# A recurrent attention layer feeding a two-matrix feed-forward layer: four reorderings in the opening stage

## The chip, the cores and the metric

The kernel runs on one core of one Trainium2 chip. The metric is device time in microseconds, the median of several executions. The engines of the core are called PE (TensorE, the matrix engine; PEld is its weight loading), DVE (VectorE), ACT (ScalarE), POOL (GpSimd) and SP (SyncE, which here only issues transfers). Each runs its own instructions strictly in the order of the program and waits at an instruction until what it needs is there. SP, ACT and POOL each have a queue of transfers of their own, and all queues are served by the same 16 DMA engines.

## The reference

```python
for t in range(S):                     # B=4, H=8, S=768, D=48
    cur = einsum('bhd,bhe->bhde', u[None] * kt, vt)
    y[:, :, t] = einsum('bhd,bhde->bhe', rt, state + cur)
    state = w[None, :, :, None] * state + einsum('bhd,bhe->bhde', kt, vt)
x = y.transpose(0, 2, 1, 3).reshape(B * S, H * D)   # 3072 x 384
h = x @ w_in                                        # 384 x 2048
out = (h * sigmoid(h)) @ w_out                      # 2048 x 384
```

A linear attention keeps one 48x48 state for each batch and head. The state is multiplied by `w` at every step and gets the outer product of `k` and `v`; the current step counts with the bonus `u` in place of the decay. The result goes through a feed-forward layer with a SiLU between its two matrices.

## The kernel before

**Units.** The sequence is cut into 6 chunks of 128 steps. A unit is one chunk of one batch: 24 units, numbered so that units 0 to 3 are the first chunk of the four batches. Inside a chunk the recurrence is written as matrix products, and only the state goes from chunk to chunk.

**Steps of a unit.** In the order text each step has a short name, with the unit's number behind it:

- `lr`, `lk`, `lv` load r, k and v (tiles `rin`, `kin`, `vin`), through SP's queue, 192 KB each (L73). For units 0 to 3 they are issued before the order begins.
- `T` turns r and then k on PE, by 8 small float32 transposes each (L251), into one of two large PSUM tiles `att`. `rT` and `kT` (L257, DVE) multiply the turned r and k by powers of w on the way out of PSUM.
- `A` is the product of r with k for two units at once (L284, PE, 64 float32 matmuls). It begins with a part of the even unit, and takes turns between the two units after that. `am` (L291, DVE) applies the causal mask.
- `ku`, `ru` (L211, L215, POOL), `rd` (L224, DVE) and `vu` (L229, POOL) make the bonus term: k times u, times r, summed over a head, times v.
- `v16` (L238, ACT) casts v to 16 bits; odd units also copy the two halves of it crosswise (`vx`, L241, L242).
- `Y` (L301, L306, PE) is the output, and `y16` (L334, DVE) adds the bonus term and casts. `yT` (L372, PE) and `xT` (L376, ACT) turn the output for the feed-forward layer.
- `kc` (L219, POOL), `S` (L318, PE) and `st` (L345, or L348 and L349, DVE) make the new state.

**The feed-forward layer.** `L` is a piece of the first product (L387, PE), `G` its SiLU (L395, ACT). The second product (L408) and the stores come later. `i_q` requests a quarter of w_in and `i_o` one of w_out, through POOL's queue, 384 KB each after a cast from float32 to float16 in the transfer (L84, L89).

**What sets the order.** The first units, up to about 45 us, follow an order written out by hand, a text of step names that a loop reads word by word (the end of the listing). It puts the instructions of every engine and queue in order. A number and a star ahead of a word mean that so many zero matmuls (128x512, tile `zs`, L161) are put on PE ahead of that step; they compute nothing. After the text a loop over pairs of units takes over, with pieces of the feed-forward layer put between them; the change does not touch that loop.

**Around the change.** `wb` spreads w over the 128 partitions with a matmul of one row (L185), `lnwb` takes its logarithm (L188, ACT), and `lamC` (L191 to L194, ACT) makes powers of w, which `kc` needs, and loads the table for the SiLU. `pads` are 8 small copies on ACT (L155) that zero the unused columns of r and k of units 4 to 7. PSUM tiles of the feed-forward layer, of `zs`, `bc`, `yp`, `sp` and `yT` share four buffers.

Of the kernel before, what the change touches and what calls it, by code (L numbers as in the profile page):

```python
# [15 lines left out]
def kernel(  # L16
# [132 lines left out]
    lamC = cst.tile([128, H, D], FP)  # L149
# [295 lines left out]
    def piece(word, f):  # L445
# [17 lines left out]
    }  # L463
    order = """
        lnw eK lamK mx clear lr4 lk4 lv4 lr5 lk5 lv5 lr6 lk6 lv6 lr7 lk7 lv7 4*T0 ku0 rT0 kT0
        4*T1 rT1 kT1 v160 ru0 rd0 ku1 wb v161 A01 ru1 am0 rd1 vu0 lnwb i_q0 lamC pads am1 vu1
        4*Y0 y160 T2 kT2 2*Y1 y161 ku2 ru2 rT2 yT0 xT0 i_q1 yT1 xT1 v162 T3 kT3 rT3 ku3 ru3 rd2
        v163 4*A23 vu2 i_q2 rd3 vu3 am2 am3 L0.0 G0.0 L0.2 G0.2 Y2 y162 Y3 y163 kc0 yT2 xT2 L0.4
        G0.4 kc1 yT3 xT3 L0.6 G0.6 S0 st0 kc2 T4 kT4 rT4 kc3 L2.0 G2.0 S1 L2.2 G2.2 st1 ku4 v164
        L2.4 G2.4 S2 L2.6 G2.6 st2 ru4 i_q3 r164 L4.8 G4.8 S3 L4.9 G4.9 st3 rd4 ku5 L4.10 G4.10  # L470
        T5 kT5 rT5 L4.11 G4.11 vu4 ru5 i_o0 A45 rd5 am4 r165 v165 L4.12 G4.12 vu5 kc4 L4.13
        G4.13 am5 sd4 kc5 Y4 S4 y164 st4 L4.14 G4.14 sd5 i_o1 Y5 S5 y165 st5 L4.15 G4.15 yT4 xT4
        yT5 xT5 T6 kT6 rT6 ku6 ru6 i_o2 H0 H1 v166 r166 H2 H3 T7 kT7 rT7 ku7 i_o3 v167 r167 H4
        ru7 rd6 stb4 stb5
# [106 lines left out]
```

## Time and profile before

| what | value |
|---|---|
| median of 5 executions | 194.7 us (194.66 to 195.44) |
| profiled execution | 195.18 us, of which the span from first to last instruction is 193.4 us |
| PE busy | 183.3 us, 95% of the span |
| POOL, ACT, DVE busy | 120.3, 108.2, 102.8 us |
| PE busy from 0 to 10, 10 to 20, 20 to 30 us | 7.53, 8.51, 8.95 us |
| PE busy from 30 to 40, 40 to 50, 50 to 60 us | 9.24, 9.23, 10.00 us |
| a load of r, k or v | 192 KB, 4.2 to 4.3 us from issue to landing (median) |
| a quarter of w_in | 384 KB, 5.9 us from issue to landing (median) |

How to read the profile: a line of the timeline gives the start, the time taken, the engine, the line of the kernel, the operation, the tile written and the tiles read, and how many instructions are merged in it; in brackets stands how long the engine sat idle before it and what released it. The letters `SPq` and `POOLq` mark the issuing of a transfer, not the transfer itself. The row of tenths cuts the span into 40 slices of 4.8 us; a 9 is 90% or more. Matmuls are pipelined, so the times of merged ones can overlap with what follows.

### The profile page before, as it was taken

What the parts mean: (1) busy time and instruction counts of PE and PEld (TensorE: products, weight loads), DVE (VectorE), ACT (ScalarE), POOL (GpSimd) and SP (SyncE); (2) the same over time, 40 slices, a digit from 0 to 9 for tenths busy, and PEclk for the clock granted to TensorE, in tenths of its full rate; (3) what the DMA queues carried; (4) which work ended last, traced back from release to release, by engine and by line L of the source; (5) the groups of instructions that cost most, each with busy time, mean ns of one, the idle gap of its engine ahead of it and who ended that gap; (6) DMA issues with size and microseconds to landing.
All of it is one profiled execution on the core that took longest, in us unless ns stands there. A gap on an engine that the chain in (4) does not pass through costs nothing.

```text
span 193.4 us, 5592 instructions
## 1 busy us (share of the span) xinstructions
PE 183.3 (95%) x2290; PEld 117.0 (61%) x2290; DVE 102.8 (53%) x188; ACT 108.2 (56%) x211; POOL 120.3 (62%) x159
## 2 busy tenths in 40 slices
PE   7788898989999999999999999999999999999992
PEld 2454684677766876665566655656755657644561
DVE  6378879855772672673673574574564355200121
ACT  5296577768380592176791276791386780199200
POOL 8489994999999939829839839739748230000000
PEclk9999999999999999999999999999999999999999
DMA  5999999999769458278177287177386201310012
GB/s 96 192 202 177 209 186 191 148 206 217 130 135 181 137 110 199 63 157 180 36 149 161 61 181 168 34 138 163 80 188 143 44 0 44 111 51 0 11 74 81
DMA packets 90123, 24.35 MB, mean 126 GB/s; under 512 B 83313, under 2 KB 90098, under 8 KB 90098
## 3 DMA queue, kind: packets, MB, share of 16 engines
q1 hardware_dynamic: 84992, 20.46, 48.8%
q0 software_dynamic: 3712, 3.15, 11.2%
q10 hardware_dynamic: 1394, 0.40, 1.0%
q8 instruction: 18, 0.29, 0.6%
q14 instruction: 7, 0.06, 0.1%
HBM read 20.65 MB, written 4.72 MB: 131 GB/s over the span
## 4 chain that ended last, share of the span: by engine, by line
PE 76%; POOL 13%; issue 4%; DMA 3%; ACT 2%; DVE 1%; ACTq 0%; POOLq 0%
PE ops L408 33%; PE hps L387 27%; PE att L284 7%; PE att L251 4%; POOL ku L211 3%; POOL kc L219 3%; DMA u_bc<-in_u_dram 3%; POOL vu L229 3%; POOL rku_f L215 2%; PE yp L306 2%; PE yp L301 2%; PE sp L318 1%; POOL win L84 1%; ACT gT L395 1%; POOL sdec L329 0%
## 5 line engine op out<-in xcount | busy, mean ns | idle before, releaser
L387 PE MATMUL hps<-xT,win 128*128 128x512 f16 (+1 forms) x360 | 68.2, 337 | 0.7 <-ACT xT L376 0.5
L395 ACT ACTIVATE gT<-hps 128x512 f16<-128x512 f32 x96 | 56.2, 598 | 18.6 <-PE hps L387 16.5
L408 PE MATMUL ops<-wout,gT 128*128 128x384 f16 x384 | 66.6, 326 | 0.0
L408 PEld LDWEIGHTS <-gT 128*128 128x128 f16 x384 | 36.3, 98 | 23.3
L387 PEld LDWEIGHTS <-win 128*128 128x128 f16 x360 | 33.2, 98 | 24.2 <-issue 1.1
L229 POOL TENSOR_TENSOR vu<-vin,rku 128x384 f32<-128x384 f32 x24 | 19.8, 830 | 28.6 <-DVE rku L224 28.6
L414 ACT COPY osb<-ops 128x384 f32<-128x384 f32 x20 | 9.6, 479 | 43.6 <-PE ops L408 39.8
L291 DVE TENSOR_TENSOR am<-att,maskM 128x1024 f16<-128x1024 f32 x12 | 14.7, 1224 | 33.4 <-PE att L284 33.4
L211 POOL TENSOR_TENSOR ku<-kin,u_bc 128x384 f32<-128x384 f32 x24 | 24.1, 1005 | 3.0 <-DMA u_bc<-in_u_dram 2.5
L215 POOL TENSOR_TENSOR rku_f<-rin,ku 128x384 f32<-128x384 f32 x24 | 24.1, 1004 | 1.7
L219 POOL TENSOR_TENSOR kc<-kin,lamC 128x384 f16<-128x384 f32 x24 | 23.9, 1003 | 0.0
L257 DVE TENSOR_TENSOR rT<-att,lamR 112x512 f32<-112x512 f32 x24 | 16.4, 685 | 11.4 <-ACT gT L395 4.0
L284 PEld LDWEIGHTS att<-rT,kT 48*64 48x64 f32 x768 | 17.9, 133 | 6.4 <-issue 4.5
L284 PE MATMUL att<-rT,kT 48*64 48x128 f32 (+1 forms) x768 | 20.5, 248 | 1.0 <-DVE rT L257 0.8
L334 DVE TENSOR_TENSOR y<-yp,vu 128x384 f16<-128x384 f32 x24 | 13.3, 556 | 13.6 <-issue 4.8
L257 DVE TENSOR_TENSOR kT<-att,lamK 112x512 f32<-112x512 f32 x24 | 16.4, 682 | 3.5 <-PE att L251 3.5
L291 DVE TENSOR_TENSOR am<-att,maskX 128x1024 f16<-128x1024 f32 x12 | 14.6, 1214 | 0.0
L238 ACT CAST v<-vin 128x384 f16<-128x384 f32 x24 | 11.5, 511 | 5.0 <-DMA vin<-in_v_dram 5.0
L416 DVE COPY osb<-ops 128x384 f32<-128x384 f32 x4 | 2.2, 558 | 21.8 <-PE ops L408 21.8
L329 POOL TENSOR_TENSOR sdec<-st,wCT 112x384 f32<-112x384 f32 x16 | 13.2, 825 | 0.0
L224 DVE TENSOR_REDUCE rku<-rku_f 128x8 f32<-128x384 f32 x24 | 12.4, 544 | 1.0 <-POOL rku_f L215 1.0
L272 ACT CAST rT<-rT 112x512 f16<-112x512 f32 x20 | 12.4, 619 | 0.3 <-DVE rT L257 0.2
(60 smaller groups left out, 161.8 us busy)
## 6 DMA issues: line engine op xcount, KB each, us to landing
rin<-in_r_dram SPq DMA_DIRECT2D x24, 192.0 KB, 4.2
vin<-in_v_dram SPq DMA_DIRECT2D x24, 192.0 KB, 4.2
out_dram<-osb SPq DMA_DIRECT2D x24, 192.0 KB, 2.2
kin<-in_k_dram SPq DMA_DIRECT2D x23, 192.0 KB, 4.3
win<-in_moe_w_in_dram POOLq DMA_DIRECT2D x4, 384.0 KB, 5.9
wout<-in_moe_w_out_dram POOLq DMA_DIRECT2D x4, 384.0 KB, 6.9
xT<-y SPq DMA_TRANSPOSE x18, 2.3
kin<-in_k_dram ACTq DMA_DIRECT2D x1, 192.0 KB, 3.6
```

The source lines that it names most:

```text
L211: nc.gpsimd.tensor_tensor(out=L(i)["ku"], in0=kin[i % NIN][:, :, 0:D], in1=u_bc, op=ALU.mult)
L215: nc.gpsimd.tensor_tensor(out=L(i)["rku_f"], in0=rin[i % NIN][:, :, 0:D], in1=L(i)["ku"], op=ALU.mult)
L219: nc.gpsimd.tensor_tensor(out=kc[i % NIN][:, :, 0:D], in0=kin[i % NIN][:, :, 0:D], in1=lamC, op=ALU.mult)
L229: nc.gpsimd.tensor_tensor(out=L(i)["vu"], in0=vin[i % NIN], in1=L(i)["rku"].unsqueeze(2).broadcast_to([128, H, D]), op=ALU.mult)
L257: nc.vector.tensor_tensor(out=L(i)[key].rearrange("p g (y t) -> p y g t", y=2), in0=L(i)["t"][0:PR, :, x], in1=lam.rearrange("p g (y t) -> ...
L284: nc.tensor.matmul(a[e][o0:o0 + HC, j, p, c0:C], kT[r0:r0 + D, p, s0:s0 + HC], rT[r0:r0 + D, p, c0:C], start=True, stop=True)
L291: nc.vector.tensor_tensor(out=am.rearrange("p h g c -> p (h g) c"), in0=L(i)["a"].rearrange("p h g c -> p (h g) c"), in1=(maskX if crossed ...
L329: nc.gpsimd.tensor_tensor(out=L(i)["sdec"], in0=st[b], in1=wCT.unsqueeze(2).broadcast_to([PR, NP, PW]), op=ALU.mult)
L334: nc.vector.tensor_tensor(out=L(i)["y16"], in0=L(i)["y"], in1=L(i)["vu"], op=ALU.add)
L387: nc.tensor.matmul(hps[:, f, :], win[:, q, (ft + f) * 128:(ft + f + 1) * 128], xts[sc][:, q, b0:b0 + nb, :].rearrange("p b t -> p (b t)"), ...
L395: nc.scalar.activation(out=gts[sc][:, ft:ft + m, b0 * C:(b0 + nb) * C], in_=hpss[b0, ft], func=AF.Silu)
L408: nc.tensor.matmul(opss[b], gts[sc][:, ft, b * C:(b + 1) * C], wout[:, ft, :], start=(ft == 0), stop=(ft == NFT - 1))
```

## The change

Only the order text changes, in four places; no instruction computes anything else than before.

- `wb` moves from ahead of the first pair product `A01` to behind it. `lnwb` moves ahead of `vu0`, and `am0` stays ahead of it; on ACT the order is as before.
- The zero matmuls: 2 instead of 4 ahead of `T1`, 4 new ones ahead of `A01`, 3 instead of 4 ahead of `Y0`, 3 instead of 2 ahead of `Y1`. In sum there are two more.
- `i_q0`, the request for the first quarter of w_in, moves on POOL from behind `vu0` to a place behind `ku1` and ahead of `ru1`. On POOL's queue nothing else moves.
- `T3` moves on PE from behind `yT1` to between `yT0` and `yT1`; `T5` moves ahead of `L4.10`. `T2` keeps its place behind `Y0` on PE. DVE's order is the same in both kernels.

```diff
-        4*T1 rT1 kT1 v160 ru0 rd0 ku1 wb v161 A01 ru1 am0 rd1 vu0 lnwb i_q0 lamC pads am1 vu1
-        4*Y0 y160 T2 kT2 2*Y1 y161 ku2 ru2 rT2 yT0 xT0 i_q1 yT1 xT1 v162 T3 kT3 rT3 ku3 ru3 rd2
+        2*T1 rT1 kT1 v160 ru0 rd0 ku1 v161 i_q0 4*A01 wb ru1 am0 lnwb vu0 rd1 3*Y0 lamC pads am1
+        vu1 T2 y160 kT2 3*Y1 y161 ku2 ru2 rT2 yT0 xT0 T3 i_q1 kT3 rT3 yT1 xT1 v162 ku3 ru3 rd2
         v163 4*A23 vu2 i_q2 rd3 vu3 am2 am3 L0.0 G0.0 L0.2 G0.2 Y2 y162 Y3 y163 kc0 yT2 xT2 L0.4
         G0.4 kc1 yT3 xT3 L0.6 G0.6 S0 st0 kc2 T4 kT4 rT4 kc3 L2.0 G2.0 S1 L2.2 G2.2 st1 ku4 v164
-        L2.4 G2.4 S2 L2.6 G2.6 st2 ru4 i_q3 r164 L4.8 G4.8 S3 L4.9 G4.9 st3 rd4 ku5 L4.10 G4.10
-        T5 kT5 rT5 L4.11 G4.11 vu4 ru5 i_o0 A45 rd5 am4 r165 v165 L4.12 G4.12 vu5 kc4 L4.13
+        L2.4 G2.4 S2 L2.6 G2.6 st2 ru4 i_q3 r164 L4.8 G4.8 S3 L4.9 G4.9 st3 rd4 ku5 T5 kT5 rT5
+        L4.10 G4.10 L4.11 G4.11 vu4 ru5 i_o0 A45 rd5 am4 r165 v165 L4.12 G4.12 vu5 kc4 L4.13
```

## The prediction

> **What bounds the kernel now.** The page comes first: TensorE (PE) is busy 95% of the span, and the busy tenths show where the rest is lost.
>
> ```profile
> span 193.4 us, 5592 instructions
> PE 183.3 (95%) x2290; PEld 117.0 (61%) x2290; DVE 102.8 (53%) x188; ACT 108.2 (56%) x211; POOL 120.3 (62%) x159
> PE   7788898989999999999999999999999999999992
> DMA  5999999999769458278177287177386201310012
> ```
>
> Apart from the last slice, PE's holes lie in the first ten, of 4.8 us each, the stage that the diff edits; there the DMA engines are busy as well. From 50 us on PE never waits (10.00 us busy of 50 to 60), so a shift of the front is carried to the end unless a later wait absorbs it. The page's chain of waits names POOL in the front, but POOL waits 2.7 us for DVE before `vu` of unit 4 at 32.38, so I follow DVE back from there. First VectorE in order of time:
>
> ```profile
> 12.12 1.22 DVE L291 TENSOR_TENSOR am<-att,maskM 128x1024 f16<-128x1024 f32 x1 [1.20 <-PE att L284]
> ...
> 15.91 0.55 DVE L334 TENSOR_TENSOR y<-yp,vu 128x384 f16<-128x384 f32 x1
> 16.38 0.68 DVE L257 TENSOR_TENSOR rT<-att,lamR 112x512 f32<-112x512 f32 x1
> 17.49 0.69 DVE L257 TENSOR_TENSOR kT<-att,lamK 112x512 f32<-112x512 f32 x1 [0.43 <-PE att L251]
> 18.09 0.68 DVE L257 TENSOR_TENSOR rT<-att,lamR 112x512 f32<-112x512 f32 x1
> 18.69 0.54 DVE L224 TENSOR_REDUCE rku<-rku_f 128x8 f32<-128x384 f32 x1
> 19.66 0.55 DVE L224 TENSOR_REDUCE rku<-rku_f 128x8 f32<-128x384 f32 x1 [0.42 <-POOL rku_f L215]
> 20.43 1.23 DVE L291 TENSOR_TENSOR am<-att,maskM 128x1024 f16<-128x1024 f32 x1 [0.22 <-PE att L284]
> ```
>
> Then PE over the same stretch:
>
> ```profile
> 15.45 0.34 PE L372 MATMUL yT<-ident,y 128*128 128x128 f16 x3
> 16.51 0.34 PE L372 MATMUL yT<-ident,y 128*128 128x128 f16 x3 [0.72 <-DVE y L334]
> 16.79 0.44 PE L251 MATMUL att<-ident,rin 64*112 64x64 f32 x8
> 17.06 0.39 PE L251 MATMUL att<-ident,kin 64*112 64x64 f32 x8
> 17.38 1.04 PE L161 MATMUL zs<-idle 128*128 128x512 f16 x4
> 18.34 2.04 PE L284 MATMUL att<-rT,kT 48*64 48x128 f32 x64
> ```
>
> The reader sees a chain. T3 (16.79, 17.06) stands behind yT1, which waits for y161. kT3 waits 0.43 us for T3; rT3 ends at 18.77; the pair product A23 ends near 20.4; am2 starts there. After it come am3, Y3 (22.85), the transposes and first-layer pieces without a pause, S0 (24.97), and VectorE solid from 25.34 to rd4 at 31.74, kT5, rT5, A45, and on through waits of 0.2 to 0.5 us. So a shift of am2 should reach the end one for one.
>
> **The change, part by part.**
>
> *T3 ahead of yT1.* y161 and rT2 end at 16.46 and 17.06 on VectorE as before. If T3 can run at about 15.9, kT3 starts at 17.06 instead of 17.49 and A23 ends near 19.95. But am2 stands behind rd3, which POOL's `rku_f` (18.61 + 1.01) releases, and that ends at 20.2. Gain: 20.43 - 20.2 = 0.23 us at most. T3 is now also the first thing PE waits on, and yT1, xT1, four zero matmuls and A23 queue behind it; xT1 has cover, as it is wanted by L0.0 after A23.
>
> *The first w_in quarter, requested behind `ku` of unit 1.* The issue costs POOL 0.93 us. It moves from 12.46 to about 10.67, the end of that `ku`. ru1 and vu0 slide by 0.9 us: ru1 ends near 12.6, before rd1 at 13.26 wants it, and vu0 near 13.4, before y160 at 14.85. vu1 still waits for rd1 until 13.80 (the 0.50 us wait that the row below shows), so POOL from vu1 on stands where it stood. On the engines this is nothing. On the transfers it is not.
>
> ```profile
> 9.64 1.01 POOL L211 TENSOR_TENSOR ku<-kin,u_bc 128x384 f32<-128x384 f32 x1
> 10.73 1.01 POOL L215 TENSOR_TENSOR rku_f<-rin,ku 128x384 f32<-128x384 f32 x1
> 11.69 0.83 POOL L229 TENSOR_TENSOR vu<-vin,rku 128x384 f32<-128x384 f32 x1
> 12.46 0.93 POOL L84 DMA_DIRECT2D win<-in_moe_w_in_dram  x1
> 13.89 0.82 POOL L229 TENSOR_TENSOR vu<-vin,rku 128x384 f32<-128x384 f32 x1 [0.50 <-DVE rku L224]
> ```
>
> Counted by queue in the trace's packet records, SP's queue moves some 50 KB each quarter microsecond until 14.25. Then the w_in packets begin, 1.8 us after the issue, and SP's queue has 23, 5, 4, 4, 4, 4, 0, 0, 0, 0 KB in the next ten quarters and is back at 45 near 17.5. The shortfall is about 2.7 us of its time; around the quarters issued at 16.69 and 20.35 it is about 2.2. Loads run one after another there, about 1.0 us each: rin3 12.53 to 13.6, kin3 from 13.60, 95% of it by 15.15, and it landed at 16.0 (11.42 + 4.6), just ahead of T3.
>
> With the issue at 10.67 the burst begins near 12.5, before rin3 rather than near the end of kin3. kin3 would end about 14.6 without a burst; add 2.2 to 2.7 for the stop: 16.8 to 17.3, and 0.9 from last packet to landing as for vin2 (12.54 to 13.4) and kin4 (21.86 to 22.8): 17.7 to 18.2. T3's second half started at 17.06 without waiting; started at 17.9 it shifts kT3, rT3, A23 and am2 by 0.85 us. `ku` of unit 3 (17.52) also waits for kin3, 0.4 us, and POOL has the 2.7 us to give.
>
> Here a rule is weighed. The Trainium skill, "DMA: Bandwidth & Descriptors", section "Queues, rings and completion order", says that a DMA engine takes turns between queues packet by packet. With equal bytes per turn the loads would run at half speed: rin3 and kin3, 384 KB at 100 KB per us from 12.5, end at 16.4 and land at 17.3, a shift of +0.25. The trace shows SP's queue at a tenth, not at half, so I stay near the row: 17.9, with +0.8 for the sum.
>
> *Zero matmuls.* Four 128x512 cost 1.04 us with their tail, 0.22 each in a row (0.26 alone). Two fewer before T1: T1 waits for rin1 (PE idled 0.60 us there), so nothing is gained. Four before the first product: T1 ends at 9.14, they end near 10.15, and the half of A01 that closes it waits for kT1 until 10.46. Nothing, unless the clock is slow. Three instead of four before Y0, behind the spread of w (0.91 us): A01 ends 12.06, spread 12.95, zeros about 13.7; am0 ends 13.34, so Y0 goes from 13.40 to some 13.6. Y0, T2, three zeros and Y1 then end near 15.6, and y161 is not due on VectorE before 15.91. Hidden, by 0.3 us; without that cover the sum would be +0.3. T2 and kT2 keep their places on PE and DVE.
>
> *Spread behind the product.* lnwb follows at 13.0 instead of 11.79 and ScalarE's chain (lamC, table load 1.28, pads) slides by 1.2: xT0 at 17.1 for 15.93. Both xT are due only at L0.0, 20.3. kc0 needs lamC at 21.96. Nothing.
>
> *T5 ahead of L4.10.* kT5 starts at 32.33, when rd4 ends; T5 was done by 32.05. PE does the same work before A45 in either order, and A45 waits for rT5. Nothing.
>
> Sum: +0.8 us from kin3, bounds -0.23 (no delay) and +1.15 (landing at 18.2), plus nothing else. The profiled execution took 195.18 for its span of 193.4, 0.48 above the median of the five; it becomes 196.0, and the median 194.7 becomes 195.5.
>
> The clock is the second rule weighed. Four zeros took 1.91 us at 2.97 and 1.04 at 6.30: PE ran at half speed until about 6 us. The Trainium skill, "TensorE: Matmul & The Clock Gate", Part 1, gives windows of about 3.4 us, an idle one returning PE to half speed, and Part 4 says transposes do not count as busy. With T3 late, zeros and Y1 end near 15.6 and the next zeros come at 18.7: 3.1 us of transposes alone. By the rows here (2.0 us between Y1's end and the next zeros, at full speed throughout) nothing is lost; by the rule it is close. If lost, A23 takes 3.1 instead of 1.55 us: +1.55 more.
>
> **Rivals.**
> 1. *The load is late enough (likeliest), 195.5.* For it: the empty quarters above, and kin3 landing only 1.1 us before it is used. Own range 195.0 to 196.0.
> 2. *Not slower: kin3 lands by 16.6.* One place, T3; the price is am2's 0.23 us gain, 194.5. It decides where kin3 lands before 17.06. For it: the edit removes the 0.43 us wait that the row shows. Against it: even equal turns land it at 17.3.
> 3. *Equal turns or a short burst:* kin3 at 17.1 to 17.4, 194.9.
> 4. *The clock falls back* in that gap, or before the first product where zeros went: 195.5 + 1.55 = 197.
>
> **How the numbers follow.** Chances: 0.60, 0.13, 0.17, 0.10. A measurement of this kernel tells about 0.3%, 0.58 us: below 194.12 is faster, above 195.28 slower. Slower: 0.85 of case 1 (0.51), all of case 4 (0.10), and 0.02 of case 3: 0.63. Faster: half of case 2, for a gain that I have not seen: 0.07. Same: 0.30. The range from 194.4 to 196.4 holds cases 1 and 3 and half of case 2; what is left out is case 4 and the rest of case 2, some 17 in 100.
>
> **What would show it.** Right: w_in packets from about 12.5, kin3 landing near 17.9, PE idle before T3's second half for that DMA, kT3 near 18.3, am2 near 21.2, rd4 near 32.6, and every row from 50 us shifted alike. Wrong: T3 done by 16.6 and am2 near 20.2; zero matmuls at 0.43 each; a later wait that swallows the shift; or POOL, not VectorE, releasing `vu` of unit 4.

## The result

The changed kernel takes 196.5 us in the median of 43 executions (195.41 to 198.97); the kernel before, measured again with 80, takes 195.25 us (194.36 to 197.99). The ratio is 1.006 with a 95% interval of 1.0045 to 1.0075: 1.2 us slower (0.9 to 1.5). Medians here are over all executions; the ratios, here and below, leave out those that took over 1.5% more than the fastest of the same kernel, and are not quotients of the medians. The forecast was slower by 0.8, to 195.5, between 194.4 and 196.4. The direction came true; the time lies 0.1 us outside the range, partly because the median of the kernel before, 194.7 over five executions, is 195.25 over eighty.

The profile after: first the busy row of the page and its row of the granted clock (in tenths of full speed), with the clock row of the kernel before under them; then PE in order of time over the stretch shown in the prediction.

```profile
span 194.2 us, 5596 instructions
PE   7797899889999999999999999999999999999992
PEclk9879999999999999999999999999999999999998
```

```profile
PEclk9999999999999999999999999999999999999999
```

```profile
15.65 0.36 PE L306 MATMUL yp<-vx,am 128*128 128x48 f16 x8
16.06 0.34 PE L372 MATMUL yT<-ident,y 128*128 128x128 f16 x3
16.33 0.43 PE L251 MATMUL att<-ident,rin 64*112 64x64 f32 x8
17.96 0.43 PE L251 MATMUL att<-ident,kin 64*112 64x64 f32 x8 [1.19 <-DMA kin<-in_k_dram]
18.32 0.34 PE L372 MATMUL yT<-ident,y 128*128 128x128 f16 x3
18.50 1.03 PE L161 MATMUL zs<-idle 128*128 128x512 f16 x4
19.46 1.87 PE L284 MATMUL att<-rT,kT 48*64 48x128 f32 x64
```

T3's first half follows yT0 at once, as the order now says. Its second half waits 1.19 us for k of unit 3 and starts at 17.96; before, it started at 17.06. VectorE shows what hangs on it:

```profile
12.73 1.22 DVE L291 TENSOR_TENSOR am<-att,maskM 128x1024 f16<-128x1024 f32 x1 [2.34 <-PE att L284]
...
16.99 0.68 DVE L257 TENSOR_TENSOR rT<-att,lamR 112x512 f32<-112x512 f32 x1
18.43 0.69 DVE L257 TENSOR_TENSOR kT<-att,lamK 112x512 f32<-112x512 f32 x1 [0.77 <-PE att L251]
...
21.38 1.22 DVE L291 TENSOR_TENSOR am<-att,maskM 128x1024 f16<-128x1024 f32 x1 [0.55 <-PE att L284]
```

The wait of kT for T3, 0.43 us before, is 0.77. am2 starts at 21.38 instead of 20.43. am0 is 0.61 us late as well (12.73 for 12.12), which has another cause: the fall of the PEclk row in its second and third slices. The four waits of PE further down, in order of time, first after and then before:

```profile
34.62 1.55 PE L284 MATMUL att<-rT,kT 48*64 48x128 f32 x60 [0.51 <-DVE rT L257]
39.47 0.34 PE L318 MATMUL sp<-v,kc 128*128 128x96 f16 x4 [0.25 <-POOL kc L219]
41.90 2.78 PE L387 MATMUL hps<-xT,win 128*128 128x256 f16 x24 [0.51 <-ACT xT L376]
46.65 1.55 PE L284 MATMUL att<-rT,kT 48*64 48x128 f32 x60 [0.25 <-DVE rT L257]
```

```profile
33.67 1.55 PE L284 MATMUL att<-rT,kT 48*64 48x128 f32 x60 [0.51 <-DVE rT L257]
38.52 0.34 PE L318 MATMUL sp<-v,kc 128*128 128x96 f16 x4 [0.25 <-POOL kc L219]
40.95 2.78 PE L387 MATMUL hps<-xT,win 128*128 128x256 f16 x24 [0.51 <-ACT xT L376]
45.70 1.55 PE L284 MATMUL att<-rT,kT 48*64 48x128 f32 x60 [0.26 <-DVE rT L257]
```

Each wait has kept its length to 0.01 us and stands 0.95 us later. Nothing between am2 and 47 us gave any of it back; 0.15 us was made up behind that, and the span grew by 0.8.

### The profile page after: what moved, and what is told of

The parts are those of the page before. It is cut to its first block, busy times and chain, and to the rows that moved or that the text cites. A ratio compares the mean times of both kernels' runs of the same rounds, so it can differ in the third digit from the quotient of the medians.

```text
span 194.2 us, 5596 instructions
## 1 busy us (share of the span) xinstructions
PE 184.2 (95%) x2292; PEld 117.8 (61%) x2292; DVE 102.8 (53%) x188; ACT 108.1 (56%) x211; POOL 120.4 (62%) x159
## 3 DMA queue, kind: packets, MB, share of 16 engines
q1 hardware_dynamic: 84992, 20.46, 48.8%
## 4 chain that ended last, share of the span: by engine, by line
PE 75%; POOL 13%; issue 4%; DMA 3%; ACT 2%; DVE 1%; ACTq 0%; POOLq 0%
PE ops L408 33%; PE hps L387 27%; PE att L284 7%; PE att L251 4%; POOL ku L211 3%; POOL kc L219 3%; POOL vu L229 3%; DMA u_bc<-in_u_dram 3%; POOL rku_f L215 3%; PE yp L306 2%; PE yp L301 2%; PE sp L318 1%; ACT gT L395 1%; POOL win L84 1%; POOL sdec L329 0%
## 5 line engine op out<-in xcount | busy, mean ns | idle before, releaser
L291 DVE TENSOR_TENSOR am<-att,maskM 128x1024 f16<-128x1024 f32 x12 | 14.7, 1224 | 34.8 <-PE att L284 34.8
L284 PEld LDWEIGHTS att<-rT,kT 48*64 48x64 f32 x768 | 18.5, 137 | 6.1 <-issue 3.9
```

The costliest lines, as they stand in the source:

```text
L284: nc.tensor.matmul(a[e][o0:o0 + HC, j, p, c0:C], kT[r0:r0 + D, p, s0:s0 + HC], rT[r0:r0 + D, p, c0:C], start=True, stop=True)
L291: nc.vector.tensor_tensor(out=am.rearrange("p h g c -> p (h g) c"), in0=L(i)["a"].rearrange("p h g c -> p (h g) c"), in1=(maskX if crossed ...
```

## The experiments

Two theories. *Late load:* the w_in packets, started before r and k of unit 3 instead of behind them, hold up that k, and T3 with all that follows. *Clock:* with zero matmuls moved, PE runs a stretch at half clock, and the slowdown is that. Each kernel below was timed beside the kernel before on the same chip. The mean granted clock is known for every execution; "whole" means 0.995 or more here. It leaves out the start (last section).

**The request alone, and everything but the request.** The first is the kernel before with one word moved, the second the changed kernel with that word back.

```diff
 request alone
-        4*T1 rT1 kT1 v160 ru0 rd0 ku1 wb v161 A01 ru1 am0 rd1 vu0 lnwb i_q0 lamC pads am1 vu1
+        4*T1 rT1 kT1 v160 ru0 rd0 ku1 i_q0 wb v161 A01 ru1 am0 rd1 vu0 lnwb lamC pads am1 vu1
 request back
-        2*T1 rT1 kT1 v160 ru0 rd0 ku1 v161 i_q0 4*A01 wb ru1 am0 lnwb vu0 rd1 3*Y0 lamC pads am1
+        2*T1 rT1 kT1 v160 ru0 rd0 ku1 v161 4*A01 wb ru1 am0 lnwb vu0 i_q0 rd1 3*Y0 lamC pads am1
```

> The kernel before with the first w_in request moved ahead of the spread of w and of ru1, and nothing else. Late-load theory: kin of unit 3 lands near 17.9, T3's second half waits for it, am2 starts near 21.3, and the kernel is 0.7 to 1.1 us slower than before. Clock rival: no difference beyond 0.2 us, since the zero matmuls are as before.

> The changed kernel with the first w_in request back behind vu of unit 0; the zero matmuls, the spread of w, T3 and T5 stay as changed. Late-load theory (the request made kin of unit 3 land at 17.9): that load lands near 16.0 again, T3's second half starts at or before 16.6, the first mask of units 2 and 3 (am2) starts at 20.2 to 20.5 where the clock holds, and the time is within 0.3 us of the kernel before. Clock rival (the zero matmuls taken from ahead of T1 cost a stretch at half clock): still 0.6 to 1.2 us above the kernel before, with am0 at 12.7 instead of 12.1.

Measured: the request alone gives 196.71 us against 195.34, ratio 1.0088 (1.0053 to 1.0123), more than I expected; of the executions with the clock whole alone the medians are 196.07 and 194.99. Everything but the request gives 195.14 against 195.34, ratio 0.9997 (0.9965 to 1.0029), with k of unit 3 landed at 16.0 and am2 at 19.75. So the one request carries the slowdown, and the other three edits together cost nothing that these runs can tell. In the profiled execution of the request alone k of unit 3 landed at 17.7, 6.6 us behind its issue at 11.16, but PE reached full clock only near 10 us there, so T3 came late for that reason too and hardly waited; this trace alone does not show the late load as the cause.

**Each of the other edits alone.** The zero matmuls with the spread of w, then T3, then T5, each in the kernel before.

```diff
 zeros and spread
-        4*T1 rT1 kT1 v160 ru0 rd0 ku1 wb v161 A01 ... 4*Y0 ... 2*Y1
+        2*T1 rT1 kT1 v160 ru0 rd0 ku1 v161 4*A01 wb ... 3*Y0 ... 3*Y1
 T3
-        yT0 xT0 i_q1 yT1 xT1 v162 T3 kT3
+        yT0 xT0 T3 i_q1 yT1 xT1 v162 kT3
 T5
-        ku5 L4.10 G4.10 T5 kT5 rT5 L4.11
+        ku5 T5 kT5 rT5 L4.10 G4.10 L4.11
```

> The kernel before with only the zero matmuls and the spread of w moved (2 ahead of T1, 4 ahead of the first product, the spread behind it, 3 ahead of Y0 and of Y1). Late-load theory: in executions whose clock holds nothing changes; in those where it falls to half behind 8.5 us, am0 starts 0.6 us later, and as no late load covers it, up to 0.6 us of it reaches the end; a mean of 0.1 to 0.4 us slower. Clock rival: the whole 1.2 us slowdown shows here.

> The kernel before with T3 ahead of yT1 and nothing else. kin of unit 3 lands at 16.0 as before; T3 ends near 16.5 and kT of unit 3 starts at 17.06 instead of 17.49; am2 starts at 20.2 instead of 20.43, held there by the bonus sum of unit 3. Time: 0.2 us faster, or the same within the interval. If T3 in that place is a loss by itself (the rival that the move of T3 costs), kT of unit 3 starts after 17.5 and the time rises.

> The kernel before with T5 ahead of L4.10 and nothing else. Every theory: no difference, since kT of unit 5 starts when the bonus sum of unit 4 ends on VectorE, and T5 is done before that in either order.

Measured: zeros 195.69 against 195.34, ratio 1.0008 (0.9981 to 1.0035); T3 195.27 against 195.34, ratio 1.0005 (0.9976 to 1.0034); T5 194.99 against 194.91, ratio 0.9993 (0.9966 to 1.002). None can be told from no change. T3 alone did in its trace what was worked out for it:

```profile
15.90 0.68 DVE L257 TENSOR_TENSOR rT<-att,lamR 112x512 f32<-112x512 f32 x1
16.50 0.68 DVE L257 TENSOR_TENSOR kT<-att,lamK 112x512 f32<-112x512 f32 x1
17.10 0.68 DVE L257 TENSOR_TENSOR rT<-att,lamR 112x512 f32<-112x512 f32 x1
17.69 0.54 DVE L224 TENSOR_REDUCE rku<-rku_f 128x8 f32<-128x384 f32 x1
19.19 0.55 DVE L224 TENSOR_REDUCE rku<-rku_f 128x8 f32<-128x384 f32 x1 [0.95 <-POOL rku_f L215]
19.66 1.22 DVE L291 TENSOR_TENSOR am<-att,maskM 128x1024 f16<-128x1024 f32 x1
```

kT3 follows rT2 without a wait, and am2 is held by the bonus sum, which waits for POOL: the cap of the gain is where it was put. am2 starts 8.02 us behind am0 here, against 8.31 in the kernel before. Further on, PE waits 0.23 us for the last quarter of w_out at 51.6 us; in the trace with only T5 moved it waits 0.52 us there. The trace of before has no such wait: PE came late enough. So what the front gains can be lost there, while a delay of the front is not made up.

The zeros alone lost the clock twice or more in 4 of 22 executions (mean clock under 0.985), and those took 199.2 to 200.8 us; in the kernel before 3 of 55 did, at 196.7 to 197.8.

**How much is asked for early, and how early.** In the first kernel only 128 of the quarter's 512 columns are requested early and the others at the old place. In the second the whole request moves half the way, behind ru1.

```diff
 128 columns early
-        ru0 rd0 ku1 wb
+        ru0 rd0 ku1 i_h0 wb
+    def ld_win_part(g):
+        cols_win(0, 128)
 half the way
-        A01 ru1 am0 rd1 vu0 lnwb i_q0 lamC
+        A01 ru1 i_q0 am0 rd1 vu0 lnwb lamC
```

> The kernel before with only the first 128 of the 512 columns of the first w_in quarter requested early (behind ku of unit 1), and the other 384 columns requested at the old place. POOL issues a transfer early, as in the changed kernel, at about the same cost to POOL, but only 96 KB follow it. If the packets are what costs: SP's loads stop for about a quarter of the time, kin of unit 3 lands 0.5 to 0.8 us later than before, and the kernel is 0 to 0.4 us slower. If the place of the issue on POOL is what costs, 1.1 us or more slower.

> The kernel before with the first w_in request moved half the way: behind ru1, ahead of vu0, about 0.9 us earlier than in the kernel before and 0.9 us later than in the changed one. Late-load theory: the w_in packets begin near 13.5, in the first third of kin of unit 3; that load lands between 16.5 and 17.7, and the kernel is 0.2 to 0.9 us slower than before. If lateness were a step and not by degrees (any request ahead of vu0 costs the same), 1.1 us or more slower.

Measured: with 128 columns, 195.35 against 194.91, ratio 0.9996 (0.996 to 1.0032), k of unit 3 landed at 16.7. POOL paid the same for the early issue as in the changed kernel:

```profile
9.52 1.00 POOL L217 TENSOR_TENSOR ku<-kin,u_bc 128x384 f32<-128x384 f32 x1
10.46 0.93 POOL L84 DMA_DIRECT2D win<-in_moe_w_in_dram  x1
11.41 1.01 POOL L221 TENSOR_TENSOR rku_f<-rin,ku 128x384 f32<-128x384 f32 x1
```

So it is the 384 KB behind the issue that cost, and not its place on POOL. Half the way gave 196.52 against 195.75, ratio 1.0014 (0.9984 to 1.0044). In its profiled execution k of unit 3 landed at 17.9, as late as with the full move and later than I expected, yet T3 did not wait, because a half-clock stretch had put PE late by itself. By degrees or as a step: these runs do not settle it.

**The early request with another order of loads.** The changed kernel, with v of unit 2 behind r and k of unit 3 on SP's queue.

```diff
-    load(2)
-    load(3)
+    ld(2, rin, r)
+    ld(2, kin, k)
+    ld(3, rin, r)
+    ld(3, kin, k)
+    ld(2, vin, v)
+    ld(3, vin, v)
```

> The changed kernel, early request and all, with the load of v of unit 2 issued behind those of r and k of unit 3 on SP's queue. Late-load theory: kin of unit 3 is then one load ahead in the queue, most of it is through before the w_in packets start, it lands by 15.5 to 16.3, T3 does not wait beyond 16.3, am2 starts near 20, and the time is that of the kernel before within 0.3 us, although the request is still early. v of unit 2 lands near 16.5 instead, with cover until 18. Rival (the early request costs by what it does on POOL, or by slowing all transfers alike): still 1 us or more slower than the kernel before.

Measured: 196.68 against 195.75, ratio 1.0031 (0.9992 to 1.007). A miss in its means: k of unit 3 landed at 18.1, although a load ahead. The w_in packets began at 13.4 in that trace and those of k of unit 3 at 13.1, so they met anyway. T3 waited 0.81 us for k, as in the changed kernel; the run does not tell the theories apart.

**The clock, with the early request kept.** The changed kernel with 4 zeros ahead of T1 again, and then with 4 more ahead of T3.

```diff
 4 ahead of T1
-        2*T1 rT1 kT1
+        4*T1 rT1 kT1
 4 more ahead of T3
-        yT0 xT0 T3 i_q1 kT3
+        yT0 xT0 4*T3 i_q1 kT3
```

> The changed kernel with 4 zero matmuls ahead of T1 again instead of 2. Late-load theory: the wait for kin of unit 3 still sets am2 near 21.3, so the time stays 1.0 to 1.4 us above the kernel before, whether the clock holds or not; the executions with a half-clock window become fewer (35 of 100 in the kernel before, 50 of 100 in the changed one). Clock rival: the time falls back to that of the kernel before.

> The changed kernel with 4 zero matmuls ahead of T1 again and 4 more ahead of T3, where PE waits for kin of unit 3. In the run with 4 ahead of T1 alone, 18 of 22 executions had a half-clock window (197.9 in the median, against 196.6 with the clock whole). If that window comes from PE having little but transposes between Y1 and the product of units 2 and 3, it becomes rare here, and the median falls by about 1.2 us; the late load stays, so the time stays 0.9 us or more above the kernel before. If the clock has another cause, the share stays.

Measured: 4 ahead of T1 gives 197.83 against 195.75, ratio 1.0097 (1.0066 to 1.0127); 18 of 22 executions lost a stretch of the clock, with a median of 198.2 (the second text above says 197.9); the four others have 196.6. Neither theory had said as much as 2 us. The trace of one follows: PE in order of time, and then two stretches. Behind the bounds and length of a stretch stand the busy us and, in brackets, the instructions of PE, PEld, DVE, ACT and POOL; then the granted clock, the DMA share and GB/s.

```profile
17.92 0.68 PE L251 MATMUL att<-ident,kin 64*112 64x64 f32 x8 [0.24 <-DMA kin<-in_k_dram]
18.53 0.50 PE L372 MATMUL yT<-ident,y 128*128 128x128 f16 x3
18.83 1.91 PE L161 MATMUL zs<-idle 128*128 128x512 f16 x4
20.67 1.80 PE L284 MATMUL att<-rT,kT 48*64 48x128 f32 x64
```

```profile
13.00:17.50 4.50, 2.71 (x48) 1.81 (x46) 3.77 (x7) 4.21 (x13) 3.95 (x5) 1.00 1.09 187
17.50:21.00 3.50, 3.26 (x31) 1.61 (x29) 2.21 (x4) 1.89 (x5) 2.53 (x3) 0.54 0.98 164
```

While it waits for the late load, PE is busy for 2.71 us of 4.50; then the clock falls, and the zeros and a part of the product behind T3 run at half speed: four zeros take 1.91 us instead of 1.03, and am2 starts at 22.52. That the little work in the wait is what lets the clock fall is tested by the second run. With 4 zeros ahead of T3 no execution of 22 lost the clock, and the kernel took 196.13 against 194.91, ratio 1.0039 (1.0017 to 1.0062). The two runs were on different chips, but on the second one the kernel before lost the clock too, in 11 of 67 executions. Its trace has the late load without any clock about it:

```profile
15.18 1.03 PE L161 MATMUL zs<-idle 128*128 128x512 f16 x4
16.77 0.43 PE L251 MATMUL att<-ident,rin 64*112 64x64 f32 x8 [0.56 <-DMA rin<-in_r_dram]
18.17 0.44 PE L251 MATMUL att<-ident,kin 64*112 64x64 f32 x8 [0.97 <-DMA kin<-in_k_dram]
```

**What cost undone, what didn't kept.** First the kernel before with the new zeros and spread but 4 ahead of T1; then the changed kernel with the request back and 4 ahead of T1.

```diff
 zeros with 4 ahead of T1
-        4*T1 ... ku1 wb v161 A01 ... 4*Y0 ... 2*Y1
+        4*T1 ... ku1 v161 4*A01 wb ... 3*Y0 ... 3*Y1
 request back, 4 ahead of T1
-        2*T1 rT1 kT1 v160 ru0 rd0 ku1 v161 i_q0 4*A01 wb ru1 am0 lnwb vu0 rd1 3*Y0
+        4*T1 rT1 kT1 v160 ru0 rd0 ku1 v161 4*A01 wb ru1 am0 lnwb vu0 i_q0 rd1 3*Y0
```

> The kernel before with the other moves of the zero matmuls and of the spread of w, but 4 zero matmuls kept ahead of T1. If taking two from ahead of T1 is what lets the clock fall for two windows (4 of 22 executions of the run that moved only the zero matmuls were above 199 us), none or few such executions are left and the time is that of the kernel before. If it is the later zeros or the spread, the share stays near one in five.

> The changed kernel with both parts that cost undone: the request back behind vu of unit 0 and 4 zero matmuls ahead of T1. T3 ahead of yT1, the later spread of w and the other zeros stay. am2 starts 0.2 to 0.4 us earlier than in the kernel before and few executions lose the clock: 0.3 to 0.8 us faster than the kernel before. If T3's place needs the early request to be of use, or the zeros do nothing, no difference.

Measured: 195.08 against 195.75, ratio 0.9954 (0.993 to 0.9978), the clock whole in 21 of 22; and 194.79 against 194.91, ratio 0.9978 (0.9955 to 1.0002), the clock whole in 22 of 22. The first is 0.9 us faster than the kernel before (0.4 to 1.4), on a chip where that one lost the clock in 24 of 67 executions: with 4 zeros kept ahead of T1 the other new ones are no loss. Its profiled execution was the one of its 22 that lost the clock (198.9 us). In that trace k of unit 3 landed at 19.5 with the request at the old place, PE waited 1.60 us for it, and the clock fell from 19.8. So the load can be late, and the clock fall behind it, without the early request; why it was so late there, one trace does not show. The second is faster than the changed kernel; against the kernel before its interval just reaches one. Beside the run with 4 more zeros ahead of T3, on the same chip and with a whole mean clock in every execution of both, it gives the cleanest price of the early request: 196.13 - 194.79 = 1.3 us, up to those four zeros, which end at 16.2 and leave PE waiting for loads.

## Why the prediction was wrong

It named the cause and the sign, and missed the size: +0.8 us where 1.2 was measured, on a level that was itself 0.55 us too low.

*The late load: right, undersized.* The step that failed reads "T3's second half started at 17.06 without waiting; started at 17.9 it shifts kT3, rT3, A23 and am2 by 0.85 us". The landing was right: 17.9 in the changed kernel, 17.7 to 18.1 in the five other traces with the full or the half-way early request. What was off is the 17.06. It came from one execution whose first loads were late: PE waited 0.60 us for r of unit 1 there. The trace with only T5 moved, whose front has the order of the kernel before, has T3's second half and am2 0.6 us earlier:

```profile
16.48 0.39 PE L251 MATMUL att<-ident,kin 64*112 64x64 f32 x8
19.86 1.23 DVE L291 TENSOR_TENSOR am<-att,maskM 128x1024 f16<-128x1024 f32 x1 [0.22 <-PE att L284]
```

In the trace of the zeros alone they start at 16.76 and 20.14. As the landing hardly moves with this, am2 shifts by 1.2 to 1.5 us. Over more traces: in the six with the request at the old place and no stretch of the clock lost, am2 starts at 20.05 in the mean (19.66 to 20.46), and in the four with the full early request and no stretch lost behind the load at 21.43 (21.18 to 21.60); the mean spans are 193.14 and 194.46. The difference, 1.4 at am2 and 1.3 in the span, agrees with the 1.3 us above and with the ratio, though these kernels differ in the other edits too. A front taken from one execution was used as if it were the typical one.

The time of that execution gave no warning: 195.18 is close to the median of eighty. A late front and an ordinary time went together because later waits differ. With only T5 moved, the front is 0.6 us earlier and the span only 0.05 us shorter, as PE waits 0.52 us for w_out.

*How the landing came about: two errors that cancelled.* The w_in packets started at 12.64, as worked out (12.5). But k of unit 3 was through at 16.33, where 16.8 to 17.3 stood, and landed 1.6 us behind its last packet, where 0.9 stood. That 17.9 came out was luck in this part.

*Equal turns against the row:* equal turns would land k at 17.3; the six traces with the early request say 17.7 to 18.1. The row was the better guide.

*POOL, the spread, T5 and the one-for-one step: right in this pair of traces.* ru1 and vu0 slid behind cover, T5 gave nothing, the spread gave nothing that was seen, and the four waits kept their lengths. That PE never waits from 50 us on holds for the traces of before and after, not for all: besides w_out, PE waits 0.16 to 0.69 us between 84 and 90 us in six of the others. vu1 waited 1.25 us instead of 0.50, since rd1 stood behind the late am0.

*T3 ahead of yT1: right in its place, not seen in the time.* The gain at am2, 0.3 us, shows in T3's own trace; so little is below what these runs can tell, and 0.23 us of it went in the wait for w_out. In the changed kernel there is none, because T3 is what waits.

*The clock: a rival at one in ten that came true in half.* Of 44 executions of the changed kernel (the profiled one with them) 22 had a mean clock below 0.995; of 189 of the kernel before on the three chips of the experiments, 54. In the trace above it was at half from 8.5 to 12 us, from ahead of the first product on; that made am0 0.61 us late, and was then hidden: T3 waited for the load anyway. Of the changed kernel's executions, those at 0.988 or 0.989 (11, like the traced one) have a median of 196.1 and those with the clock whole 196.4. The 6 at 0.991 have 197.2 and the 5 below 0.985 have 198.0; that their lost stretch lies at A23 is likely from the run with 4 ahead of T1, but no trace of them shows it. In that run it moved am2 by about 1 us (22.52, beside 21.38 and 21.60), not by the 1.55 worked out for A23. So the clock makes the tail of the changed kernel, not its slowdown, and the sum had no part for it.

*The level.* 0.55 us of the miss is the kernel before itself, which my range did not allow for. Applied to 195.25, the forecast of +0.8 would have been 196.05.

## What to carry to other kernels

Before a transfer is requested earlier, list what is queued on the other queues in that stretch and which of it is used just in time: here a free slot on POOL moved a burst of 384 KB in front of a load that had 1 us to spare (landed at 16.1, used at 17.06). Where a wait is to be compared with a landing, take the start of what waits for it from several traces; the landing stayed while the start varied by 0.6 us. Zero matmuls that are to keep the clock up belong where PE waits longest, and a new wait for a transfer makes such a place: 18 of 22 executions lost the clock without them there, none of 22 with them.

## What the runs showed of the hardware

While the packets of a w_in quarter are served, SP's queue is not halved but all but stopped. By the packet records it moves some 50 KB each quarter microsecond until 12.75 in the changed kernel, then 0 to 10 KB in each quarter from 13.0 to 15.0, and 48 again at 16.0. Counted in order, the last packet of k of unit 3 lay 1.2 to 1.6 us ahead of its landing in all six traces with the early request. With the request back it lay 1.9 us ahead (14.1 and 16.0), although the burst began only behind it, at 14.7. The 0.9 us of v of unit 2 is thus no rule for loads near a burst; what draws out the landing these records do not show.

The lost stretches of the clock lasted 3.4 us each in the packed clock records. One followed a stretch of that length, from 5.1 to 8.5 in the changed kernel, in which PE did two zero matmuls (0.60 us) beside its transposes; in the run with 4 ahead of T1 another followed the stretch from 14.4 to 17.8 with a zero or two, Y1 and transposes. So PE need not be idle throughout for the clock to fall. The Trainium skill, "TensorE: Matmul & The Clock Gate", Part 1, speaks of an idle window of about 3.4 us; the length agrees, and a window holding 0.6 us of plain matmuls counted as idle enough here.

The mean clock of an execution does not show a late warm start: in the traces of the request alone and of the request back with 4 ahead of T1, PE ran at half speed until about 10 us, and the mean is given as 1.0.
